# Attention's first two pairs in the written order: 12 fillers, late factors, order kept on four engines

## The chip, the cores and the metric

One NeuronCore of a Trainium2 chip runs the whole program. Its five engines each work through their own instructions in order: PE (TensorE, matrix products and transposes), DVE (VectorE), ACT (ScalarE, here exponentials, copies and casts), POOL (GpSimd) and SP (SyncE, which issues transfers). They wait for each other by semaphores. The metric is the device time of one execution, in microseconds, median of several runs; lower is better.

## The reference

Three layers follow each other, all in float32:

```
scores = (q @ k.T) / sqrt(64), causal         # 4 x 8 heads, 576 tokens of 64
local  = softmax(scores) @ v
phi    = elu(q) + 1
mem    = (phi @ M_prev) / (phi @ z_prev + 1e-6)
g      = sigmoid(beta)                        # one number a head
x      = g * mem + (1 - g) * local            # 2304 tokens x 512
x      = (silu(x @ w_gate) * (x @ w_val)) @ w_out
P      = sinkhorn(x @ moe2_w_gate), 8 rounds  # 8 experts
out    = sum over e of P[:, e] * (relu(x @ w1[e]) @ w2[e])
```

The change touches the attention alone, the first of the three.

## The kernel before

Attention is worked off in pairs of heads, 16 pairs in all. Each float32 operand of a product is split into a high and a low part (QH and QL, KH and KL, and so on), and a product is three products of parts: high with high, high with low, low with high. Keys and queries stand in blocks of 128 columns; because of the causal mask block 4 has scores of 576 columns, block 3 of 448, block 2 of 320 (with block 0, of 64, beside it) and block 1 of 192.

For one pair the work goes through these steps, each a generator that is advanced a piece at a time:

- L, `load`: the transfers of q and k (tile qk), of v and the memory (vm) and of z and q (zq). Then ACT makes QH and KH, POOL the low part KL; then DVE makes QL; then POOL splits the memory (vmr).
- Q, `prepare`: ACT makes the parts of phi (tile ph) in two activations; DVE adds them, multiplies with z (pz), sums (nb) and takes the reciprocal; POOL scales phi by it.
- S, `scores`: PE makes the scores of a block into a tile ps of PSUM, DVE takes the negated maximum (nm), ACT the exponential (tiles P, and E for block 0) with the row sums (sums). Two tiles ps exist, so the scores of a block wait for the exponentials of the block before the last.
- N, `normalize`: DVE makes factors from the sums, POOL scales the exponentials by them.
- V, `transposed`: PE transposes the scaled exponentials and phi into tiles pt of PSUM, of which three exist; ACT or DVE copies them out (T, F, Z).
- W, `values`: PE multiplies with v and the memory into po; ACT copies the result into xacc.

DVE's factors use beta: `gates` loads beta and moe2's gate weights (at the list's place 1) and, in its second half, makes eb, g and the table gs with one exponential on ACT, four operations of 8 columns, ten small copies on DVE, and the split of the gate weights (wgs).

Which piece comes when is a written list. BEGIN stands for the first two pairs and the loads of the third ("S0" is the next piece of scores of pair 0; "X33" is 33 filler products of a mask tile with itself into the unused bank po, which nothing reads). ORDER is one round of the loop, run for pairs 2 to 15, in which pieces of a pair and of its two neighbours are interleaved. END closes. `schedule` joins them.

The list is the order in which the program is written down; a scheduler then orders each engine's instructions itself, unless an instruction is recorded with `keep_in_program_order`. The wrapper class `Ordered` does that for every call on the four engines PE, ACT, DVE and POOL while `self.steady` is true. In the kernel before this is so from the first piece behind BEGIN and one whole ORDER, so from the second round of the loop on; before that the scheduler decides. The early conversions of the next layer's weights (step C) run in attention too.

Behind attention the gated layer begins, with the conversion of its weights on DVE (`load_units`, tied behind attention's last move on DVE), and then the experts' layer, which takes most of the time. Most lines of attention are recorded under line 93, the wrapper's call.

Of the kernel before, what the change touches and what calls it, by code (L numbers as in the profile page):

```python
# [42 lines left out]
ORDER = """  # L43
# [4 lines left out]


BEGIN = """  # L50
    L0 L0 Q0 X33 L1 L0 L0 S0 L2 X5 Q0 S0 S0 X5 S0 X7 X9 Q0 Q0 L1 Q1 L1 K0 X7 L1 S0 X5 Q1 N0 Q0 X7 X7 Q1
    V0 S0 S1 Q1 S1 S1 N0 V0 V0 V0 V0 V0 S1 S1 L2 Q1 L2 V0 W0 N0 W0 V0 V0 V0 S1 L2 V0 N1 N1 N1 W0
"""
END = """
# [1 line left out]
    U-1 U-1 U-1 U-1 U-1 U-1 U-1  # L56
"""

FIRST = 6

COPIES = "AAAAVVAVAVA"

# [1 line left out]
def schedule(n):  # L64

    steps = lambda text, base: [(s[0], base + int(s[1:])) for s in text.split()]
    middle = [(s, i + LAG[s]) for i in range(2, n) for s in ORDER.split() if i + LAG[s] < n]
    return steps(BEGIN, 0) + middle + steps(END, n)


def joined(steps, *counts):

    for n in counts:
        for _ in range(n):
            next(steps)
        yield
# [86 lines left out]
class Kernel:  # L163
# [34 lines left out]
    def attention(self, after=None):  # L198
        tc = self.tc
        nc = self.nc = Ordered(tc.nc, tc, lambda: self.steady)  # L200
        with ExitStack() as st, ExitStack() as first:
            pool = lambda n, b, to=st, **k: to.enter_context(tc.tile_pool(name=n, bufs=b, reuse_waits="tile", **k))

            self.s1, self.s2 = (pool(f"s{n}", n, first, side="right") for n in (1, 2))
            self.a1, self.a2, self.a3, self.a4 = (pool(f"a{n}", n) for n in (1, 2, 3, 4))
            self.pss = pool("pss", 2, space=PSUM)
            self.pst = pool("pst", 3, space=PSUM)
            self.pso = pool("pso", 1, space=PSUM)
            a1 = self.a1
            self.identb = self.s1.tile([P, P], BF16, name="identb")  # L210
            nc.vector.tensor_copy(self.identb, self.ident)

            self.mask = self.s1.tile([P, P], BF16, name="mask")
            nc.gpsimd.memset(self.mask, 0.0)
            nc.gpsimd.affine_select(
                out=self.mask, in_=self.mask, compare_op=ALU.is_ge, fill=MASKED,
                base=0, pattern=[[1, P]], channel_multiplier=-1,
            )
            self.mask0 = self.s1.tile([P, 2, 64], BF16, name="mask0")
            nc.gpsimd.memset(self.mask0, 0.0)  # L220
            for j in range(2):
                self.masked = nc.vector.tensor_copy(self.mask0[0:64, j], self.mask[0:64, 0:64])
            busy = self.pso.tile([P, 512], F32, name="po")

            self.P0 = []
            for n in range(2):
                t = a1.tile([P, 2, D], F32, name=f"P0{n}")
                nc.vector.memset(t, 0.0)
                self.P0.append(t)

            pairs = [(b, hp) for b in range(B) for hp in range(NP)][:self.n_pairs]
            n = len(pairs)
            live = [dict(b=b, hp=hp, P0=self.P0[hp % 2]) for b, hp in pairs]
            early = self.early()
            for p in live:
                p["steps"] = {
                    "L": self.load(p), "Q": self.prepare(p), "S": self.scores(p), "N": self.normalize(p),
                    "V": self.transposed(p), "W": self.values(p),
                }
                if p in live[:2]:  # L240
                    p["steps"]["S"] = joined(p["steps"]["S"], 2, 1, 2, 2, 2)
                if p is live[0]:
                    p["steps"]["V"] = joined(p["steps"]["V"], *10 * [1], 2)
                p["steps"].update({k: p["steps"][v] for k, v in SAME.items()})
                p["steps"]["C"] = early
            done = object()
            steps = schedule(n)
            for nth, (step, at) in enumerate(steps):
                self.steady = len(BEGIN.split()) + len(ORDER.split()) <= nth
                if nth == len(steps) - len(END.split()) and after:  # L250
                    self.ahead = self.load_units()
                    next(self.ahead)
                if nth == 1:
                    gates = self.gates()
                    next(gates)
                if nth == FIRST:
                    with tc.issue_after(self.low_q.ins):
                        next(gates, None)
                if step == "X":
                    for _ in range(at):  # L260
                        nc.tensor.matmul(busy[:, 0:P], self.mask, self.mask, start=True, stop=True)
                else:
                    next(live[at]["steps"][step], done)
            self.nc, self.steady = tc.nc, False
            first.close()
            if after:
                self.open_early(after)

                with tc.issue_after(self.last_exp.ins):
                    for _ in range(2):  # L270
                        next(self.ahead)
                    self.xs = self.split_x(*CHUNKS1[0])
# [1364 lines left out]
```

## Time and profile before

| what | value |
|---|---|
| median of 3 runs | 2102.82 us (2101.58 to 2103.69) |
| profiled execution, own time | 2105.53 us |
| its span, first to last instruction | 2103.7 us |
| PE busy, share of the span | 2067.0 us, 98% |
| DVE busy | 1716.7 us, 82% |
| ACT busy | 974.1 us, 46% |
| POOL busy | 521.4 us, 25% |
| mean granted clock of PE | 0.997 |

Shares of busy time are means over very different stages. The start of the program, the first 50 us of 2100, has to be read from the timelines. PE's clock has two levels here, 2.4 GHz (granted 1.00) and 1.2 GHz (0.50); a stretch between the two held both.

### The profile page before, as it was taken

The page shows a single profiled execution, that of the slowest core. Times are in us where ns is not written, and L with a number is a line of the kernel's source. Part 1 is how long each engine was busy: PE and PEld are TensorE (multiplying, and loading weights), DVE is VectorE, ACT ScalarE, POOL GpSimd, SP SyncE. Part 2 cuts the span into 40 slices and gives each one's busy share as a digit, 9 for nine tenths or more (in the row PEclk, how much of TensorE's full clock was granted, in tenths as well). Part 3 has the DMA queues.
Part 4 walks back from the last instruction along what each step waited for, and adds up shares of the span by engine and source line. Part 5 has one row for each costly group of instructions (what it writes and reads, how often), then busy time and mean ns, then how long its engine had stood idle before and what let it go on. Part 6 is the DMA issues. An engine that isn't in the chain of part 4 may idle for free.

```text
span 2103.7 us, 40585 instructions
## 1 busy us (share of the span) xinstructions
PE 2067.0 (98%) x15848; PEld 1907.4 (91%) x15848; DVE 1716.7 (82%) x3193; ACT 974.1 (46%) x1912; POOL 521.4 (25%) x458
## 2 busy tenths in 40 slices
PE   7999999999999999999999999999999999999999
PEld 5666787877889889999999999999999999999998
DVE  7899899675454668898888888888889888898887
ACT  6999543443333324444434444444444444444432
POOL 6888544000000042122121221212212122121210
PEclk9999999999999999999999999999999999999999
DMA  5342587476587747656566564665647656575564
GB/s 191 111 142 85 186 288 260 142 251 209 170 285 275 271 130 250 209 172 241 167 236 212 169 234 166 232 201 191 230 163 241 204 186 231 167 240 203 183 212 159
DMA packets 123359, 425.77 MB, mean 202 GB/s; under 512 B 13600, under 2 KB 13600, under 8 KB 120096
## 3 DMA queue, kind: packets, MB, share of 16 engines
q1 hardware_dynamic: 121728, 417.93, 59.3%
q10 hardware_dynamic: 1440, 5.24, 0.6%
q8 instruction: 126, 2.06, 0.4%
q14 instruction: 65, 0.53, 0.1%
HBM read 374.36 MB, written 48.76 MB: 201 GB/s over the span
## 4 chain that ended last, share of the span: by engine, by line
PE 71%; DVE 8%; DMA 4%; issue 1%; ACT 1%; SPq 0%; DVEq 0%; ACTq 0%
PE pu L1447 16%; PE pc L1284 15%; PE pq L1447 11%; PE pt L1284 10%; PE po L559 5%; PE pt L1370 4%; PE p L559 3%; PE pc L559 3%; PE pq L559 2%; DMA xr<-xp 2%; PE pt L559 2%; DMA xp<-xl 2%; DVE m L1300 2%; DVE xacc L1453 2%; DVE h L1269 1%; DVE h L1266 1%
## 5 line engine op out<-in xcount | busy, mean ns | idle before, releaser
L1447 PE MATMUL pu<-xl,h 128*128 128x256 f32 x3240 | 424.7, 278 | 2.6 <-DVE xacc L1453 2.1
L1447 PEld LDWEIGHTS pu<-xl,h 128*128 128x128 f32 x3240 | 393.0, 188 | 6.9 <-DVE xacc L1453 3.8
L1284 PE MATMUL pc<-xr,w 128*128 128x256 f32 x3048 | 390.5, 277 | 3.9 <-DMA xr<-xp 3.8
L1284 PEld LDWEIGHTS pc<-xr,w 128*128 128x128 f32 x3048 | 367.3, 188 | 7.2 <-issue 4.4
L1447 PE MATMUL pq<-xl,h 128*128 128x256 f32 x2430 | 317.1, 277 | 0.0
L1447 PEld LDWEIGHTS pq<-xl,h 128*128 128x128 f32 x2430 | 294.1, 188 | 0.4
L1284 PE MATMUL pt<-xr,w 128*128 128x256 f32 x2280 | 291.0, 277 | 0.0
L1268 ACT CAST h<-m 128x512 fp32r<-128x512 f32 (+1 forms) x345 | 190.4, 556 | 200.8 <-DVE m L1300 193.1
L1284 PEld LDWEIGHTS pt<-xr,w 128*128 128x128 f32 x2280 | 274.2, 188 | 0.7
L1453 DVE SCALAR_TENSOR_TENSOR xacc<-pu,Pw,xacc 128x256 f32<-128x256 f32 x540 | 237.1, 475 | 39.3 <-PE pu L1447 39.1
L1291 ACT COPY m<-pc 128x512 f32<-128x512 f32 x192 | 111.9, 583 | 249.6 <-PE pc L1284 245.7
L1453 DVE SCALAR_TENSOR_TENSOR xacc<-pq,Pw,xacc 128x256 f32<-128x256 f32 x405 | 177.5, 474 | 47.0 <-PE pq L1447 47.0
L1269 DVE TENSOR_TENSOR h<-m,h 128x512 fp32r<-128x512 f32 (+1 forms) x345 | 207.4, 625 | 1.5
L1189 POOL TENSOR_TENSOR ws<-raw 128x512 f32<-128x512 f32 x60 | 80.8, 1356 | 507.8 <-DMA raw<-w 165.6
L1265 ACT ACTIVATE h<-m 128x512 fp32r<-128x512 f32 x192 | 121.4, 633 | 172.3 <-DVE m L1296 164.9
L1300 DVE SCALAR_TENSOR_TENSOR m<-m 128x512 f32<-128x512 f32 x240 | 185.5, 773 | 14.2 <-ACT m L1327 10.6
L1296 DVE TENSOR_TENSOR m<-pt,m 128x512 f32<-128x512 f32 x192 | 131.3, 684 | 53.0 <-ACT m L1291 52.2
L559 PE MATMUL p<-xs,gw 128*128 128x512 f32 (+1 forms) x864 | 171.1, 355 | 3.4 <-ACT hf L796 1.3
L559 PEld LDWEIGHTS p<-xs,gw 128*128 128x128 f32 x864 | 142.3, 188 | 30.7 <-DVE hf L797 2.8
L1266 DVE SCALAR_TENSOR_TENSOR h<-m,h 128x512 fp32r<-128x512 f32 x192 | 150.3, 783 | 12.1 <-ACT h L1265 11.7
L1176 POOL TENSOR_TENSOR w<-raw,w 128x512 fp32r<-128x512 f32 x15 | 38.8, 2584 | 428.9 <-ACT w L1175 428.9
L559 PE MATMUL po<-h,ws 128*128 128x512 f32 x576 | 144.4, 391 | 0.2 <-DVE h L817 0.2
(232 smaller groups left out, 2956.9 us busy)
## 6 DMA issues: line engine op xcount, KB each, us to landing
xr<-xp SPq DMA_DIRECT2D x476, 512.0 KB, 4.2
raw<-w SPq DMA_DIRECT2D x64, 512.0 KB, 7.4
gw<-kg SPq DMA_DIRECT2D x24, 1024.0 KB, 7.0
graw<-gvo SPq DMA_DIRECT2D x36, 512.0 KB, 4.4
kg<-gw SPq DMA_DIRECT2D x24, 512.0 KB, 4.2
ws<-ko SPq DMA_DIRECT2D x24, 512.0 KB, 3.9
xp<-xl SPq DMA_DIRECT2D x21, 512.0 KB, 5.2
qk<-qkv SPq DMA_DIRECT2D x16, 640.0 KB, 5.2
```

Source lines behind the costliest of these rows:

```text
L559: self.nc.tensor.matmul(out, lhs[a], rhs[b], start=start and n == 0, stop=stop and n == 2, skip_group_check=shared)
L1265: nc.scalar.activation(hi, src, AF.Relu)
L1266: self.later(1, lambda: nc.vector.scalar_tensor_tensor(lo, src, 0.0, f32(hi), op0=ALU.max, op1=ALU.subtract))
L1268: nc.scalar.copy(hi, src)
L1269: self.later(1, lambda: nc.vector.tensor_sub(lo, src, f32(hi)))
L1284: self.marks[3] = nc.tensor.matmul(out[:, j * HT:(j + 1) * HT], w[:, a, j, k], x[:, b, k], start=start and j + k + n == 0, stop=k + n == 3 ...
L1291: self.marks[1] = nc.scalar.copy(t, src)
L1296: nc.vector.tensor_add(t, a, b)
L1300: relu = lambda out, a, b, op: nc.vector.scalar_tensor_tensor(out, a, 0.0, b, op0=ALU.max, op1=op)
L1370: nc.tensor.matmul(ph[:, j * HT:(j + 1) * HT], w[:, b, j, k], x[:, c, k], start=j + a + k + m == 0, stop=a + k + m == 4, skip_group_check= ...
L1447: nc.tensor.matmul(po[:, c], h[a][:, x, j, c * P:(c + 1) * P], w2[b][:, y, j], start=start and c + j + n == 0, stop=j + n == 3, skip_group ...
L1453: self.marks[2] = nc.vector.scalar_tensor_tensor(acc, po[:, c], self.Pw[:, at, e:e + 1], acc, op0=ALU.mult, op1=ALU.add)
```

## The change

Three edits, all in the start of attention. BEGIN has 12 fillers where it had 33. FIRST, the place in the list at which the second half of `gates` is written, is 18 where it was 6. And `self.steady` is true from the first piece, so that the four engines keep the written order in BEGIN and in the first round of the loop too. One line that sets it is added before the loop.

```
 BEGIN = """
-    L0 L0 Q0 X33 L1 L0 L0 S0 L2 X5 Q0 S0 S0 X5 S0 X7 X9 Q0 Q0 L1 Q1 L1 K0 X7 L1 S0 X5 Q1 N0 Q0 X7 X7 Q1
+    L0 L0 Q0 X12 L1 L0 L0 S0 L2 X5 Q0 S0 S0 X5 S0 X7 X9 Q0 Q0 L1 Q1 L1 K0 X7 L1 S0 X5 Q1 N0 Q0 X7 X7 Q1
     V0 S0 S1 Q1 S1 S1 N0 V0 V0 V0 V0 V0 S1 S1 L2 Q1 L2 V0 W0 N0 W0 V0 V0 V0 S1 L2 V0 N1 N1 N1 W0
 """
-FIRST = 6
+FIRST = 18
             steps = schedule(n)
+            self.steady = True
             for nth, (step, at) in enumerate(steps):
-                self.steady = len(BEGIN.split()) + len(ORDER.split()) <= nth
+                self.steady = True
```

What this does to the engines is seen in the order of their instructions, below for three places. Buffer numbers differ between the two programs, so the same tile has another number.

On DVE, from pair 1's QL to pair 0's first maxima, before:

```order
L93 SCALAR_TENSOR_TENSOR QL<-qk,QH 128x640
L93 RECIPROCAL g_218<-g_218 128x8
L93 TENSOR_REDUCE nb<-pz 128x10
L93 COPY gs<-g_218 64x4
L93 COPY gs<-g_218 128x4 x4
L93 COPY gs<-g_218 64x4
L93 COPY gs<-g_218 128x4 x4
L93 TENSOR_REDUCE nm_256<-ps 128x1
L93 TENSOR_REDUCE nm_258<-ps 128x1
```

and with the change, from behind pair 0's QL to the first copy into gs:

```order
L93 TENSOR_REDUCE nm_215<-ps 128x1
L93 TENSOR_REDUCE nm_217<-ps 128x1
L93 SCALAR_TENSOR_TENSOR ph<-zq,ph 128x640
L93 TENSOR_REDUCE nm_242<-ps 128x2
L93 TENSOR_REDUCE nm_266<-ps 128x1
L93 TENSOR_REDUCE nm_261<-ps 128x2
L93 TENSOR_TENSOR pz<-ph,zq 128x640
L93 TENSOR_SCALAR eb<-eb 128x8
L93 RECIPROCAL g_295<-eb 128x8
L93 TENSOR_SCALAR g_295<-g_295 128x8
L93 RECIPROCAL g_295<-g_295 128x8
L93 COPY gs<-g_295 64x4
```

The two maxima nm of pair 0's 576-column block stand directly behind its QL now, and the factors (eb, g, gs) behind all maxima of pair 0 but the last; pair 1's QL, which stood ahead of gs, stands behind all of it.

On POOL, from pair 0's phi on, before (P_239, P_285, P_310 and P_371 are pair 0's blocks from 576 to 192 columns, P_151 the place of its block 0, E_313 that block's exponentials):

```order
L93 TENSOR_TENSOR ph<-ph,nb 128x640
L93 TENSOR_SCALAR P_239<-P_239,sums 128x576 x2
L93 TENSOR_SCALAR P_285<-P_285,sums 128x448 x2
L93 TENSOR_TENSOR ph<-ph,nb 128x640
L93 TENSOR_TENSOR KL<-qk,KH 128x640
L93 TENSOR_SCALAR P_310<-P_310,sums 128x320 x2
L93 TENSOR_SCALAR P_151<-E_313,sums 64x64 x2
L93 TENSOR_SCALAR P_371<-P_371,sums 128x192 x2
```

and with the change (the same blocks are P_198, P_244, P_269 and P_350, and E_272):

```order
L93 TENSOR_TENSOR KL<-qk,KH 128x640
L93 TENSOR_SCALAR P_198<-P_198,sums 128x576 x2
L93 TENSOR_SCALAR vmr<-vm 128x256
L93 TENSOR_TENSOR vmr<-vm,vmr 128x256
L93 TENSOR_SCALAR P_244<-P_244,sums 128x448 x2
L93 TENSOR_TENSOR ph<-ph,nb 128x640
L93 TENSOR_SCALAR P_269<-P_269,sums 128x320 x2
L93 TENSOR_TENSOR KL<-qk,KH 128x640
L93 TENSOR_TENSOR ph<-ph,nb 128x640
L93 TENSOR_SCALAR P_151<-E_272,sums 64x64 x2
L93 TENSOR_SCALAR P_350<-P_350,sums 128x192 x2
```

The first KL of the lower rows is pair 1's, the second pair 2's. In both orders pair 2's KL and pair 1's phi stand ahead of the scaling of pair 0's E and 192-column block; KL stands behind the 320-column block now, where it stood ahead of it.

On ACT, from the end of pair 0's exponentials on, before (P_413 is pair 1's first block; QH and KH here are pair 2's):

```order
L93 ACTIVATE P_310,sums<-ps,nm_302 128x320 x2
L93 ACTIVATE E_313,sums<-ps,nm_307 128x64
L93 ACTIVATE QH<-qk 128x640
L93 CAST KH<-qk 128x640
L93 ACTIVATE P_371,sums<-ps,nm_369 128x192 x2
L93 COPY T<-pt 128x4x128 x2
L93 ACTIVATE P_413,sums<-ps,nm_430 128x576
```

and with the change, from pair 1's last exponentials (E_482, P_495) to pair 2's first (P_578):

```order
L93 ACTIVATE E_482,sums<-ps,nm_476 128x64
L93 ACTIVATE P_495,sums<-ps,nm_493 128x192 x2
L93 ACTIVATE QH<-qk 128x640
L93 CAST KH<-qk 128x640
L93 COPY T<-pt 128x128
L93 COPY Z_529<-pt 64x64 x2
L93 COPY F_380<-pt 128x64
L93 CAST Z<-pt 128x512
L93 COPY xacc<-po 128x512
L93 ACTIVATE ph<-zq 128x640
L93 ACTIVATE ph<-ph 128x640
L93 ACTIVATE P_578,sums<-ps,nm_595 128x576
```

Pair 2's QH and KH stand behind all of pair 1's exponentials now, before they stood behind pair 0's E. The copy into xacc of pair 0 and both activations of phi stand ahead of pair 2's first exponential.

On SP one load of values (vm) stands earlier and one load of zq later; the transfers are the same.

## Rows read from the trace of the kernel before

**Rows 1.** The page, share of the span by engine: busy us, share, instructions.

```profile
PE 2067.0 (98%) x15848; PEld 1907.4 (91%) x15848; DVE 1716.7 (82%) x3193; ACT 974.1 (46%) x1912; POOL 521.4 (25%) x458
```

**Rows 2.** Busy time by stretch: length, each engine, granted clock, DMA.

```profile
core 0: us, PE busy (x) PEld busy (x) DVE busy (x) ACT busy (x) POOL busy (x), PEclk, DMA share, GB/s
...
18.00:20.00 2.00, 2.00 (x15) 1.18 (x11) 2.00 (x4) 0.23 (x3) 1.02 (x1) 0.53 1.01 410
...
24.00:26.00 2.00, 2.00 (x13) 1.51 (x12) 1.61 (x2) 2.00 (x7) 2.00 (x3) 0.77 0.23 93
...
61.70:74.40 12.70, 12.41 (x100) 8.59 (x102) 10.43 (x22) 12.08 (x35) 11.56 (x16) 1.00 0.40 116
260.00:280.00 20.00, 20.00 (x90) 16.58 (x89) 19.55 (x33) 8.07 (x13) 10.10 (x5) 1.00 0.89 298
```

**Rows 3.** Timeline of PE, start: start us, length us, what, xcount, idle before.

```profile
6.56 0.61 PE L93 MATMUL ps<-KH,QH 64*128 64x288 f32 x2 [6.56 <-ACT KH L93]
7.10 3.70 PE L93 MATMUL po<-mask 128*128 128x128 bf16 x33
10.73 0.61 PE L93 MATMUL ps<-KL,QH 64*128 64x288 f32 x2
11.14 0.37 PE L93 MATMUL ps<-KH,QL 64*128 64x288 f32 x2
...
11.96 2.06 PE L93 MATMUL po<-mask 128*128 128x128 bf16 x34
17.43 0.47 PE L93 MATMUL ps<-KH,QH 64*128 64x448 f32 x2 [3.42 <-ACT P L93]
...
24.71 0.49 PE L93 MATMUL ps<-KH,QH 64*128 64x288 f32 x1
...
25.86 0.61 PE L93 MATMUL pt<-ident,P 128*128 128x128 f32 x4
...
36.32 0.41 PE L93 MATMUL ps<-KH,QH 64*128 64x288 f32 x2
...
48.90 0.40 PE L93 MATMUL ps<-KH,QH 64*128 64x288 f32 x2
```

**Rows 4.** Timeline of DVE, start.

```profile
5.92 0.83 DVE L93 SCALAR_TENSOR_TENSOR QL<-qk,QH 128x640 fp32r<-128x640 f32 x1 [3.85 <-ACT QH L93]
...
13.54 2.32 DVE L93 COPY gs<-g 64x4 f32<-64x4 f32 x10
15.77 1.41 DVE L93 TENSOR_REDUCE nm<-ps 128x1 f32<-128x576 f32 x2
```

**Rows 5.** Timeline of POOL, start.

```profile
6.59 1.56 POOL L93 TENSOR_TENSOR KL<-qk,KH 128x640 fp32r<-128x640 f32 x1 [4.80 <-ACT KH L93]
...
22.25 2.70 POOL L93 TENSOR_SCALAR P<-P,sums 128x576 f32<-128x576 f32 x4 [2.01 <-DVE nb L93]
...
26.69 1.55 POOL L93 TENSOR_TENSOR KL<-qk,KH 128x640 fp32r<-128x640 f32 x1
...
29.60 0.72 POOL L93 TENSOR_SCALAR P<-E,sums 64x64 f32<-64x64 f32 x2
30.41 0.82 POOL L93 TENSOR_SCALAR P<-P,sums 128x192 f32<-128x192 f32 x2
...
43.40 1.26 POOL L93 TENSOR_TENSOR ph<-ph,nb 128x640 f32<-128x640 f32 x1 [0.36 <-DVE nb L93]
```

**Rows 6.** Timeline of ACT, start.

```profile
23.43 0.74 ACT L93 ACTIVATE QH<-qk 128x640 fp32r<-128x640 f32 x1
...
35.93 0.27 ACT L93 COPY T<-pt 128x128 f32<-128x128 f32 x1
...
37.73 0.75 ACT L93 ACTIVATE ph<-ph 128x640 f32<-128x640 f32 x1
39.33 0.74 ACT L93 ACTIVATE P<-ps,nm 128x576 f32<-128x576 f32 x1 [0.84 <-DVE nm L93]
...
40.77 0.58 ACT L93 COPY xacc<-po 128x512 f32<-128x512 f32 x1
```

## The prediction

> **What bounds the kernel now.** I read first the page's share of each engine, then the busy time by stretch, then the timelines of the first 50 us engine by engine. The page has PE busy for 98% of the span [rows 1]. The stretches show where that is true: in a settled round of attention PE works 12.41 of 12.70 us [rows 2], and further on, where the expert weights are converted, DVE is the engine without a gap, 19.55 of 20 us. Both stretches come behind the start, follow it in a fixed order and hold no slack, so a start that ends D us later or earlier moves the end by D. The question is therefore one of place: when do pair 3's first score products, the first that stand in a settled round, begin? Before, at 48.90 us [rows 3].
>
> In the start itself nothing is full. PE runs 33 fillers while KL has long been there (KL ends at 6.59 + 1.56 = 8.15 [rows 5], KL's first product waits until 10.73 [rows 3]), stands still for 3.42 us before 17.43, and then runs at half clock: 0.53 granted of full speed in 18 to 20 us, back at 0.77 in 24 to 26 [rows 2]. The reader is to see in these rows a chain that goes round all four engines: score products (PE), negated maximum (DVE), exponential (ACT), scaling (POOL), transposes (PE). What counts is what stands in front of each link on its engine.
>
> **The change part by part.** Three edits, one effect that matters: in the first two pairs and in the first round of the loop the four engines' instructions now stand as the list BEGIN writes them. I lay the new order on the durations of the rows, link by link.
>
> First maximum. KH is ready as before, at 6.56 PE starts [rows 3]; the fillers are over by then, since they wait for the mask alone: 12 at 3.70/33 = 0.11 each is 1.3 us in time when PE had nothing else, so their removal costs nothing there. KL's products start at 8.15. Five groups of two products follow, four at 11.14 - 10.73 = 0.41 and one at 7.10 - 6.56 = 0.54, plus 0.6 for the last one's own length and 0.1 of masks: the scores stand at about 11.1. DVE has nothing ahead of the maximum any more, where before the ten copies into gs (13.54, 2.32 long) kept it until 15.77 [rows 4]. Gain so far: 4.7 us.
>
> Pair 0's exponentials. From that maximum to the end of the last exponential of this block, behind which QH starts, it took 23.43 - 15.77 = 7.7 us [rows 4, 6]. The order within is nearly the same, so they end at 11.1 + 7.7 = 18.8.
>
> Pair 1's start, where the gain goes. Before, ACT had made pair 1's QH and KH, and DVE the factors, while the first scores were in the making. Now QH and KH stand on ACT behind pair 0's exponential, and on DVE the factors stand between that exponential and pair 1's QL: four small operations (at the 0.23 of a gs copy, 0.9), the ten copies (2.3), wgs (0.2), the sum into nb and QL (0.8 each, as QL's 0.83 [rows 4]). That is 5.0 us, so 23.8 to 24.0; pair 0's sums come next (two small ones, 0.4), then POOL scales the first block (2.70 for four, 0.7 for the first [rows 5]), then PE transposes four blocks (0.61 [rows 3]). Pair 1's first scores: 24.0 + 0.4 + 0.7 + 0.5 = 25.6, against 24.71 before. The 4.7 us are spent, and 0.9 more.
>
> Pair 1 to its last exponential. Before: 35.93 - 24.71 = 11.2 us [rows 3, 6], with pair 3's QH and KH inside (two of 0.74, 1.4 with their overlap), which now come later: 9.8. On the other side PE's scores of 320 and 192 columns now stand behind pair 0's transposes, whose bank of PSUM is given back by ACT only after both 448-column exponentials: four copies and casts of about 0.5 (the 0.58 of a 512-column copy [rows 6]) and eight transposes at 0.15 that were spread over waiting time now stand in line, 3 us. Bounds: 0 (they still hide) and 3; I take 3, since copy, transposes and scores are each behind the other in the new order. End: 25.6 + 9.8 + 3.0 = 38.4.
>
> Pair 2's preparation, now on the path. Before, ACT cast pair 2's QH at 23.43 and POOL made KL at 26.69 [rows 5, 6]; E0's and the 192-column block's scaling followed at 29.60 and 30.41. In the new order QH and KH stand behind pair 1's last exponential, and on POOL, as before, KL and the scaling of phi stand ahead of pair 0's last scalings: what cost nothing while KL was early now holds them. PE has nothing more to do until those are done, as transposes of the 192-column block are next on it. So: QH and KH 1.4, KL 1.55, phi 1.26, E0 twice 0.72, the first 192-column block 0.41 [rows 5]: 38.4 + 5.3 = 43.7. PE has run dry at about 37, a wait of some 6.7 us that the trace of before does not have.
>
> To pair 2's first exponential. Before, from pair 2's scores to the copy of pair 0's output it took 40.77 - 36.32 = 4.45 us [rows 3, 6]; now eight transposes (1.2) and four products of 256 columns (0.6, taken as four transposes) stand ahead of them on PE: 6.2 us, to 49.9. And the exponential, which before stood ahead of that copy (39.33 against 40.77), now stands behind it and behind both activations of phi: 0.58 and two of 0.75, less 0.1 of overlap at neighbours, 1.9 [rows 6]. So 51.8 where it was 39.33: +12.5 us. From here on the order is the settled one, and pair 3 follows at the old distance, 48.90 - 39.33 = 9.6, at 61.4.
>
> The clock. 34 fillers took 2.06 us at full speed, 61 ns each, against 112 ns for the 33 before them [rows 3]: 2.4 and 1.2 GHz. Before, a stretch of 3.42 us without a product was followed by half speed until about 25 us [rows 2, 3]. A wait of 6.7 us will do at least that, so the 6.2 us from 43.7 on run at half clock until it comes back. Bounds: 0 (all of it hidden behind DVE and ACT) and 6.2 (all at half clock and all on the path); at half speed for 6.2 us, about as long as in before, PE does 3.1 us of work and loses 3.1, of which the exponential's wait for the output copy keeps most: I take 2.
>
> The transfers move little: SP issues one load of values earlier and one zq later, and no chain above waits for either.
>
> Sum: -4.7 + 5.6 (pair 1 late by 0.9) + 11.6 (pair 2's exponential late by 12.5) + 2.0 (clock) = +14.5 us. The profiled execution took 2105.5 us round a span of 2103.7, so 2120.0 by its own time; it lay 2.7 above the median of the runs shown, so the median to expect is 2117. Ends of the terms: without the 3.0 and the clock, +9.5; with the whole 6.2 of clock, +18.7.
>
> The Trainium skill (TensorE: Matmul & The Clock Gate, Part 1: The HAM clock gate) has half speed as the state at rest, lifted by the array's own activity. The trace agrees that the first 33 fillers ran at half speed and the next 34 did not. By that rule 21 fewer fillers and longer waits put the lifting off; that is rival A.
>
> **The rivals.** A: PE stays at 1.2 GHz through the whole start and into the first settled rounds. For it: 0.53 granted after a wait of half the length now expected [rows 2]; against it: the settled rounds keep PE at 12.41 of 12.70, and the clock came back by 26 us before. It costs the 6.2 above, 1 to 2 us more in pair 0 and pair 1, and half a round at half speed: +20 to +25, 2123 to 2128.
>
> B, the other side: the wait on POOL never gets to PE, because pair 1's exponentials come early enough. Its place is QH of pair 2 on ACT, its price the 4.7 us kept from the first maximum: 2098. It decides if that QH starts no later than about 29 us, ten before my 38.4, so that E0's scaling is done when PE wants it. For it: the engines are half idle in the start; against it: pair 1's QL cannot come before the factors, and that link alone eats the 4.7.
>
> C: a late start is swallowed where DVE converts weights. If that stretch waited for its loads and not for DVE, it would end at the same time, 2103. Against it: 19.55 of 20 us busy [rows 2], and the loads are issued as DVE frees their tiles.
>
> D: the change does not do what it says, the scheduler's order staying. The rows of the order show that it is another on three engines, so I give it nothing of its own.
>
> **How the numbers follow.** Forecast (new wait on POOL, +9.5 to +18.7): 0.80. A: 0.08. B: 0.05. C: 0.05. The rest, 0.02, lies nearer no change. A measurement of this kernel tells about 0.2%, 4.2 us, from no change. Slower by over that: forecast and A, 0.88. Within it: C and one of the rest, 0.06. Faster: B and one of the rest, 0.06. The likeliest case's own range is 2112 to 2121; the ends are let out by 2 and 1 for queueing that no row shows: 2110 to 2122.
>
> **What would show it.** In the new profile: the first maximum on DVE near 11 us and gs near 20 (right: the first two links); pair 1's first scores on PE between 25 and 27; KL of pair 2 on POOL near 40, and a wait of PE of 5 to 8 us that a POOL scaling ends, about 37 to 44; half clock granted in the stretch behind it; pair 2's first exponential at 50 to 55, behind the copy into xacc; pair 3's first scores at 59 to 65 and rounds of 12.7 us as before; the stretch of DVE's conversions as long as before. If PE has no such wait, or pair 3's scores begin before 55 us, the forecast is wrong in its main step; if they do begin late and the end does not move, C holds.

## The result: slower by 0.71%, and the profile after

| | before | after |
|---|---|---|
| median, six runs of each side by side | 2103.26 us | 2120.70 us |
| ratio, with its 95% interval | | 1.0071 [1.0054, 1.0088] |
| profiled execution, own time | 2105.53 us | 2121.88 us |
| its span | 2103.7 us | 2120.1 us |

The ratio is 14.9 us of 2103 [11.4, 18.5]; the two profiled executions lie 16.4 us apart. The page has the same work as before: PE's busy time grew by 6.4 us against [rows 1], all other engines by 4 at most, up or down.

```profile
PE 2073.4 (98%) x15827; PEld 1910.9 (90%) x15827; DVE 1712.8 (81%) x3193; ACT 974.4 (46%) x1912; POOL 523.6 (25%) x458
```

So the time is waiting, and some slow products: no engine got more to do. From the timeline of PE (start us, length us, engine, line, what, count, idle time before it and what ended it), the rows that answer to [rows 3]:

```profile
8.15 0.61 PE L93 MATMUL ps<-KL,QH 64*128 64x288 f32 x2 [1.03 <-POOL KL L93]
...
24.67 1.11 PE L93 MATMUL pt<-ident,P 128*128 128x128 f32 x4 [3.91 <-POOL P L93]
25.71 0.61 PE L93 MATMUL ps<-KH,QH 64*128 64x288 f32 x2
...
45.73 1.09 PE L93 MATMUL pt<-ident,P 128*128 128x128 f32 x3 [5.38 <-POOL P L93]
...
56.54 0.47 PE L93 MATMUL ps<-KH,QH 64*128 64x448 f32 x2 [1.93 <-ACT P L93]
...
64.96 0.40 PE L93 MATMUL ps<-KH,QH 64*128 64x288 f32 x2
77.64 0.40 PE L93 MATMUL ps<-KH,QH 64*128 64x288 f32 x2
```

Pair 3's first scores, the first inside a settled round, come at 64.96 us where they came at 48.90: 16.06 later, which is the difference of the spans (16.4) within 0.4. Pair 4's follow 12.68 us on. The same row of the kernel before, for use below:

```profile
61.58 0.40 PE L93 MATMUL ps<-KH,QH 64*128 64x288 f32 x2
```

Both pairs are late by the same 16.06. PE has a wait of 5.38 us that it did not have, ahead of 45.73, and POOL's timeline shows what it waits for:

```profile
41.69 1.55 POOL L93 TENSOR_TENSOR KL<-qk,KH 128x640 fp32r<-128x640 f32 x1 [7.85 <-ACT KH L93]
43.20 1.25 POOL L93 TENSOR_TENSOR ph<-ph,nb 128x640 f32<-128x640 f32 x1
44.44 0.72 POOL L93 TENSOR_SCALAR P<-E,sums 64x64 f32<-64x64 f32 x2
45.25 0.83 POOL L93 TENSOR_SCALAR P<-P,sums 128x192 f32<-128x192 f32 x2
```

Pair 0's 192-column block, at 45.25, stands behind E0, that behind phi (43.20), that behind pair 2's KL (41.69), and KL waited 7.85 us for KH. ACT says why KH was late, and what stands ahead of pair 2's first exponential:

```profile
32.44 0.63 ACT L93 ACTIVATE P<-ps,nm 128x448 f32<-128x448 f32 x1 [2.31 <-DVE nm L93]
33.06 0.63 ACT L93 ACTIVATE P<-ps,nm 128x448 f32<-128x448 f32 x1
...
38.14 0.53 ACT L93 ACTIVATE P<-ps,nm 128x320 f32<-128x320 f32 x1 [2.64 <-DVE nm L93]
...
39.85 0.43 ACT L93 ACTIVATE P<-ps,nm 128x192 f32<-128x192 f32 x1
...
40.24 0.75 ACT L93 ACTIVATE QH<-qk 128x640 fp32r<-128x640 f32 x1
...
53.78 0.59 ACT L93 COPY xacc<-po 128x512 f32<-128x512 f32 x1 [5.26 <-PE po L93]
...
55.67 0.72 ACT L93 ACTIVATE P<-ps,nm 128x576 f32<-128x576 f32 x1
```

QH and KH follow at once on pair 1's last exponential (39.85), and the exponential at 55.67 follows on the copy into xacc, for which ACT stood still for 5.26 us, and on phi. DVE at the start, answering to [rows 4]:

```profile
9.98 1.42 DVE L93 TENSOR_REDUCE nm<-ps 128x1 f32<-128x576 f32 x2 [3.28 <-PE ps L93]
...
19.63 2.30 DVE L93 COPY gs<-g 64x4 f32<-64x4 f32 x10
```

Last the stretches (length; busy time of PE, PEld, DVE, ACT, POOL; granted clock; DMA), the last two answering to [rows 2]:

```profile
24.00:26.00 2.00, 1.33 (x6) 1.00 (x8) 1.97 (x5) 1.09 (x5) 2.00 (x3) 0.50 1.02 399
46.00:48.00 2.00, 2.00 (x10) 1.53 (x11) 0.29 (x1) 0.96 (x5) 1.19 (x3) 0.50 0.24 97
58.00:60.00 2.00, 2.00 (x13) 1.34 (x11) 1.78 (x5) 2.00 (x5) 1.00 (x1) 0.50 0.65 167
77.64:90.34 12.70, 12.41 (x101) 8.59 (x100) 10.43 (x22) 12.10 (x35) 11.58 (x16) 1.00 0.37 117
260.00:280.00 20.00, 20.00 (x90) 16.55 (x89) 19.56 (x34) 7.95 (x14) 8.82 (x5) 1.00 0.87 278
```

PE runs at 1.2 GHz at 24 to 26, 46 to 48 and 58 to 60; a settled round is 12.41 of 12.70 us as before, and DVE's conversions fill 19.56 of 20 us as before. So the loss lies in the first 65 us: 16.06 of the 16.4 are there when pair 3 begins.

### The profile page after: what moved, and what is told of

It is laid out like the page before. It is cut to its first block, busy times and chain, and to the rows that moved or that the text cites. A ratio compares the mean times of both kernels' runs of the same rounds, so it can differ in the third digit from the quotient of the medians.

```text
span 2120.1 us, 40534 instructions
## 1 busy us (share of the span) xinstructions
PE 2073.4 (98%) x15827; PEld 1910.9 (90%) x15827; DVE 1712.8 (81%) x3193; ACT 974.4 (46%) x1912; POOL 523.6 (25%) x458
## 4 chain that ended last, share of the span: by engine, by line
PE 67%; DVE 11%; DMA 5%; issue 1%; ACT 1%; SPq 0%; ACTq 0%; DVEq 0%
PE pu L1448 15%; PE pc L1285 14%; PE pq L1448 10%; PE pt L1285 10%; PE po L560 4%; PE pt L1371 4%; PE pc L560 3%; PE p L560 3%; DMA xr<-xp 2%; DVE xacc L1454 2%; PE pq L560 2%; DVE m L1301 2%; DMA xp<-xl 2%; PE pt L560 2%; DVE h L1270 1%; DVE h L1267 1%
```

## The experiments

Eleven kernels. The theories: O, the order kept in BEGIN costs the time by the chain just read; R, the order kept in the loop's first round; C and K, the fillers and the clock; F, the late factors; the rival W of two runs is named with them. "Shift" is how much later than 61.58 pair 4's first scores stand, the first round in which every kernel runs at full clock.

| kernel | ratio to before, 95% interval | in us | pair 3's scores | shift |
|---|---|---|---|---|
| the change | 1.0071 [1.0054, 1.0088] | +14.9 | 64.96 | +16.06 |
| before, 12 fillers | 1.0016 [1.0003, 1.0029] | +3.4 | 53.81 | +5.71 |
| before, late factors | 0.9995 [0.9984, 1.0007] | -1.1 | 49.38 | +1.21 |
| change, 33 fillers, early factors | 1.0079 [1.0059, 1.0099] | +16.6 | 65.72 | +16.84 |
| change, order kept behind BEGIN | 1.0020 [1.0008, 1.0031] | +4.2 | 53.34 | +4.44 |
| before, first round kept | 1.0021 [1.0010, 1.0033] | +4.4 | 52.08 | +4.28 |
| change, order kept in BEGIN alone | 1.0073 [1.0056, 1.0090] | +15.3 | 63.20 | +14.30 |
| change, pair 2's QH, KH early | 1.0065 [1.0049, 1.0080] | +13.7 | 61.03 | +12.13 |
| change, scaling ahead of KL | 1.0037 [1.0022, 1.0052] | +7.8 | 59.62 | +10.72 |
| change, waits filled | 1.0062 [1.0047, 1.0077] | +13.0 | 61.73 | +12.83 |
| before, 80 fillers more | 1.0005 [0.9994, 1.0016] | +1.1 | 52.38 | +3.49 |
| change, three causes away | 1.0042 [1.0026, 1.0058] | +8.8 | 57.08 | +8.17 |

Over all twelve the time follows the shift one for one: time less shift lies between -2.9 and +1.6 us, -0.7 in the mean, and eleven of the twelve shifts lie inside the interval of their time (the twelfth is the run with 80 fillers more). What the start loses, the kernel loses. A shift is read from one profiled execution of its kernel. In these PE's first score products stand between 6.00 and 6.56 us, as the first load of q and k landed, so half a us of a shift can be the load and not the edit.

### Which edit: fillers alone

```
-    L0 L0 Q0 X33 L1 ...
+    L0 L0 Q0 X12 L1 ...
```

> The kernel before with one edit alone: 12 fillers in place of 33. Theory O (the written order kept in the first two pairs costs the time, by pair 2's QH and KH behind pair 1's exponentials): pair 3's first scores within 1 us of the 48.90 of before, since the first maximum waits for the factors on DVE until 15.8 anyway; ratio 0.998 to 1.002. Rival C (the missing fillers leave PE at half speed for longer): pair 3's first scores 5 us or more later, ratio 1.003 or more. Rival F (the late factors cost it) says as O here.

Pair 3's scores came at 53.81, the ratio is 1.0016 [1.0003, 1.0029]: theory O missed, and C had the direction, with less than it asked for (4.9 us of 5, 1.0016 of 1.003). Pair 1's first scores still stand at 24.68, but PE stays at half speed there, from 18.1 to 35.2 us:

```profile
24.68 0.61 PE L93 MATMUL ps<-KH,QH 64*128 64x288 f32 x1
...
36.28 0.36 PE L93 MATMUL ps<-KH,QH 64*128 64x192 f32 x2
```

and so its stretches say:

```profile
24.00:26.00 2.00, 2.00 (x9) 1.67 (x8) 0.71 (x2) 1.22 (x5) 2.00 (x3) 0.50 0.29 116
30.00:32.00 2.00, 2.00 (x11) 1.36 (x10) 1.35 (x2) 0.95 (x2) 1.28 (x4) 0.50 0.40 164
```

The same products, from those scores to pair 1's 192-column scores, take 11.6 us (24.68 to 36.28) without a wait; before it was 7.4 (24.71 to 32.14, full speed from 25). That is 4.2 us of the 5.71; the rest comes at 52 to 56, at half speed once more. So with the scheduler's order the 21 fillers are worth some 5 us of start by way of the clock, which I had priced at nothing. The scheduler also moved other instructions when the fillers went, so this run is not fillers alone on every engine.

### Which edit: late factors alone

```
-FIRST = 6
+FIRST = 18
```

> The kernel before with one edit alone: the second half of the gates at place 18 of the list in place of 6. Theory O (the kept order costs it): the order on each engine is still the scheduler's, which may put the factors where it likes; pair 3's first scores within 1.5 us of 48.90, ratio 0.998 to 1.002. Rival F (factors that come later hold pair 1's QL and pair 0's scaling, and so everything behind): pair 1's first scores 2 us or more later than 24.71, pair 3's 5 us or more later, ratio 1.003 or more. Rival C (fillers and clock) says no change here.

49.38 and 0.9995 [0.9984, 1.0007]: as O said. In the scheduler's order late factors alone cost nothing that can be told, and F falls.

### Which edit: the kept order alone

```
-    L0 L0 Q0 X12 L1 ...
+    L0 L0 Q0 X33 L1 ...
-FIRST = 18
+FIRST = 6
```

> The changed kernel with 33 fillers and the factors at place 6 again, so that of the three edits the kept order stands alone. Theory O: the wait of PE that a scaling on POOL ends is still there (5 us or more, between 37 and 47 us), pair 3's first scores at 62 to 66 where the changed kernel has 64.96; ratio to before 1.005 to 1.009. Rivals C and F (fillers, factors): with both edits undone the start is as before, pair 3's first scores below 55, ratio 0.998 to 1.003.

Pair 3's scores came at 65.72, the ratio is 1.0079 [1.0059, 1.0099], the change's own loss. The wait that a scaling on POOL ends is 5.12 us, ahead of 45.67, as O said. The kept order alone does it, and under it the other two edits together make no difference that can be told (+16.84 against +16.06); what each of them does under it was not run apart.

### Which part of the order

The order kept only from the first round on, with the change's other edits, and with none of them; then the order kept in BEGIN alone:

```
+                self.steady = len(BEGIN.split()) <= nth
```

> The changed kernel with the written order kept on the four engines only behind BEGIN, from the first piece of the loop's first round on; BEGIN itself stands in the scheduler's order again, with 12 fillers and the late factors. Theory O puts the loss into BEGIN (pair 2's QH and KH there): pair 2's QH on ACT at 23 to 27 us again, no wait of PE of over 4 us behind 30 us, pair 3's first scores at 47 to 51; ratio to before 0.998 to 1.003. Rival R (the kept order of the loop's first round costs it, by the copy into xacc and both activations of phi ahead of pair 2's first exponential): pair 2's first exponential 5 us or more later than 39.33, pair 3's scores at 55 or later, ratio 1.003 or more.

> The kernel before with one edit alone: the written order kept on the four engines from the loop's first round on; BEGIN in the scheduler's order, 33 fillers, the factors at place 6. Theory R (the first round's kept order, with the copy into xacc and phi ahead of pair 2's first exponential, costs 1 to 2 us, and half speed did the rest in the kernel with 12 fillers): pair 2's first exponential at 40.5 to 41.5 where it was 39.33, pair 3's first scores at 49.5 to 51, ratio 0.999 to 1.002. Rival (the kept round costs the 4.4 us which the kernel with BEGIN in the scheduler's order had lost): pair 3's scores at 52.5 or later, ratio 1.001 to 1.004.

```
+                self.steady = not len(BEGIN.split()) <= nth < len(BEGIN.split()) + len(ORDER.split())
```

> The changed kernel with the loop's first round in the scheduler's order again, the written order kept in BEGIN alone (12 fillers, late factors). Theory O (BEGIN's order costs it): PE's wait that a scaling on POOL ends is still 4 us or more, pair 2's first exponential stands ahead of the copy into xacc again, and pair 3's first scores come at 60 to 64, ratio to before 1.004 to 1.007. Rival R (the first round's kept order is what costs): pair 3's scores below 55, ratio 1.003 or less.

Both kernels with the first round kept missed their forecasts. In the first, pair 3's scores came at 53.34, between O's 51 and R's 55, with a ratio as O had it and pair 2's first exponential at 44.09, 4.8 us late where R asked for 5. In the second, the exponential came at 42.09 and pair 3's scores at 52.08, both later than theory R had them and the scores earlier than its rival's 52.5, with a ratio as the rival had it. So the kept first round by itself costs some 4 us (+4.28), and the rows of that second kernel show two parts. On ACT:

```profile
40.19 0.59 ACT L93 COPY xacc<-po 128x512 f32<-128x512 f32 x1 [4.18 <-PE po L93]
...
42.09 0.72 ACT L93 ACTIVATE P<-ps,nm 128x576 f32<-128x576 f32 x1
```

on PE:

```profile
42.95 0.47 PE L93 MATMUL ps<-KH,QH 64*128 64x448 f32 x2 [1.93 <-ACT P L93]
```

and by stretch:

```profile
42.00:44.00 2.00, 1.04 (x10) 0.73 (x10) 1.66 (x3) 2.00 (x6) 0.00 (x0) 1.00 0.00 2
46.00:48.00 2.00, 2.00 (x12) 1.67 (x11) 1.85 (x5) 2.00 (x7) 2.00 (x2) 0.50 0.24 94
```

ACT waits 4.18 us for the product that the copy into xacc takes, with pair 2's first exponential behind it, which comes at 42.09 in place of 39.33 [rows 6]. And behind a wait of PE of 1.93 us the clock is at half from 44.4 to 54.6 us, while PE is busy throughout. What that adds is seen in the first of the two kernels (change, order kept behind BEGIN). It has the same wait, and from its end to pair 4's first scores the same instructions in the same order on all four engines, but at full speed:

```profile
44.95 0.47 PE L93 MATMUL ps<-KH,QH 64*128 64x448 f32 x2 [1.93 <-ACT P L93]
```

```profile
46.00:48.00 2.00, 2.00 (x21) 1.51 (x19) 1.93 (x4) 2.00 (x5) 0.59 (x1) 1.00 0.48 126
```

From the end of the wait to pair 4's first scores it takes 21.07 us there (44.95 to 66.02) and 22.91 here (42.95 to 65.86): half speed is 1.8 of the 4.28, and the wait alone does not bring it. That the two kernels lose about the same (+4.44 and +4.28) is chance: the first, with 12 fillers, had half speed earlier, from 19.5 to 33.2 us, and its copy into xacc stands at 42.19, 2.0 later than here.

BEGIN's order alone costs +14.30, nearly the whole; pair 2's exponential stood ahead of the copy again (51.49 against 55.21), as O said. The wait that a scaling on POOL ends came out at 2.10 us, ahead of 45.90, where O had 4 or more: pair 2's scores now stand ahead of it on PE, with waits of their own for KH and KL (1.08 and 1.25 us). The parts do not add up: 14.3 and 4.3 are 18.6, and together they cost 16.1. Where they overlap was not tried.

### The links of the chain, one by one

Pair 2's QH, KH and KL moved ahead of pair 1's scores; then instead the scaling of E0 and the 192-column block moved ahead of KL (second line of BEGIN):

```
-    V0 S0 S1 Q1 S1 S1 N0 V0 V0 V0 V0 V0 S1 S1 L2 Q1 L2 V0 W0 ...
+    V0 S0 L2 S1 Q1 S1 S1 N0 V0 V0 V0 V0 V0 S1 S1 Q1 L2 V0 W0 ...
```

> The changed kernel with one piece moved in the list: pair 2's QH, KH and KL stand right behind pair 0's first transposes and last scores, ahead of pair 1's scores, where they stood behind pair 1's last exponentials. Theory O (PE's wait at 40.3 to 45.7 comes from pair 2's KL on POOL, which waits for KH on ACT): KL starts near 25 and no longer ends that wait, the wait shrinks from 5.4 to 2 to 3 us since the scaling of pair 0's E and 192-column block now waits for phi and its own place only; pair 3's first scores at 60 to 62 instead of 64.96, ratio to before 1.004 to 1.006 where the changed kernel had 1.0071. Rival W (the wait is due to the order of the scalings alone, or to pair 1's long exponentials): the wait stays at 5 us or more and the ratio at 1.007.

```
-    ... S1 S1 L2 Q1 L2 V0 W0 N0 W0 ...
+    ... S1 S1 N0 L2 Q1 L2 V0 W0 W0 ...
```

> The changed kernel with one piece moved in the list: the scaling of pair 0's E and 192-column block on POOL stands ahead of pair 2's QH, KH and KL; QH and KH stay behind pair 1's last exponentials. Theory O (the scaling waits for KL, not for its own data): the wait of PE that ended at 45.73 is gone or under 1.5 us, pair 2's scores then wait for KL (ready near 43.2) instead, so pair 3's first scores come at 60 to 62 in place of 64.96, ratio to before 1.004 to 1.006. Rival W (the scaling's own data are late): wait and ratio stay.

In the first, KL starts at 29.58 (25 was expected) and the wait shrinks from 5.38 to 1.65 us, more than expected, while the ratio, 1.0065, lies just above the 1.006 expected; on POOL the scaling now waits for phi, and phi for DVE:

```profile
29.58 1.54 POOL L93 TENSOR_TENSOR KL<-qk,KH 128x640 fp32r<-128x640 f32 x1
...
38.94 1.71 POOL L93 TENSOR_TENSOR ph<-ph,nb 128x640 f32<-128x640 f32 x1 [5.61 <-DVE nb L93]
```

and on PE:

```profile
41.93 1.09 PE L93 MATMUL pt<-ident,P 128*128 128x128 f32 x3 [1.65 <-POOL P L93]
```

In the second the scaling runs straight behind the 320-column block, and no wait of PE over 0.84 us is left there:

```profile
33.40 0.72 POOL L93 TENSOR_SCALAR P<-E,sums 64x64 f32<-64x64 f32 x2
34.22 0.83 POOL L93 TENSOR_SCALAR P<-P,sums 128x192 f32<-128x192 f32 x2
```

Pair 3's scores at 59.62 and the ratio of 1.0037 are better than expected. The two give back 3.9 and 5.3 us of shift, of which 0.5 and 0.4 are the earlier first load (PE's first scores at 6.02 and 6.11, in the change at 6.51). The wait was made by what stood ahead of the scaling on POOL, not by its data.

### The clock in the new waits

```
-    ... X7 X7 Q1
+    ... X7 X57 Q1
-    ... W0 N0 W0 V0 V0 V0 S1 ...
+    ... W0 N0 W0 H45 V0 V0 V0 S1 ...
...
+                elif step == "H":
+                    for _ in range(at):
+                        nc.tensor.matmul(self.po[:, 0:P], zero, self.mask, start=False, stop=False)
...
```

> The changed kernel with fillers in two of PE's waits: 50 more products of the mask ahead of the wait that ended at 24.67, and 45 products with a zero tile, added into pair 0's output where they add nothing, ahead of the wait that ended at 45.73. No other engine's order moves. Theory K (beside the order, half speed behind the new waits costs 3 to 4 us of the +16): granted clock 1.00 in 24 to 33 and in 46 to 50, pair 3's first scores at 61 to 63.5 in place of 64.96, ratio to before 1.005 to 1.0065. Rival (half speed there lies beside DVE's and ACT's work and costs nothing): clock up, pair 3's scores and the ratio as in the changed kernel, within 0.5 us. If the fillers themselves hold PE up, the scores come later than 64.96.

61.73, as K said; the ratio is 1.0062 [1.0047, 1.0077]. The clock was up in 46 to 50 as expected, but in 24 to 33 only until 29.6. By stretch:

```profile
24.00:26.00 2.00, 1.78 (x18) 1.36 (x18) 1.97 (x4) 1.30 (x5) 2.00 (x3) 1.00 1.06 416
30.00:32.00 2.00, 1.58 (x8) 1.18 (x7) 0.23 (x2) 2.00 (x6) 1.04 (x2) 0.50 0.00 0
46.00:48.00 2.00, 2.00 (x22) 1.28 (x20) 1.50 (x6) 0.40 (x1) 0.49 (x1) 1.00 0.00 0
```

PE from pair 1's first scores on:

```profile
24.80 0.40 PE L93 MATMUL ps<-KH,QH 64*128 64x288 f32 x2
...
44.27 0.84 PE L93 MATMUL pt<-ident,P 128*128 128x128 f32 x3 [2.18 <-POOL P L93]
```

ACT, the two parts of pair 1's stage and the copy:

```profile
30.00 0.64 ACT L93 ACTIVATE P<-ps,nm 128x448 f32<-128x448 f32 x1 [1.59 <-DVE nm L93]
30.63 0.63 ACT L93 ACTIVATE P<-ps,nm 128x448 f32<-128x448 f32 x1
...
36.68 0.53 ACT L93 ACTIVATE P<-ps,nm 128x320 f32<-128x320 f32 x1 [3.38 <-DVE nm L93]
...
50.49 0.59 ACT L93 COPY xacc<-po 128x512 f32<-128x512 f32 x1 [4.09 <-PE po L93]
```

From the end of the wait to the copy it took 6.22 us (44.27 to 50.49), in the change 8.05 (45.73 to 53.78): half speed behind the new wait costs 1.8 us. In pair 1, from the first scores to the 448-column exponentials, it took 5.20 (24.80 to 30.00) at full speed, in the change 6.73 (25.71 to 32.44) at half: 1.5 more. Half speed came back from 29.6 to 39.8, and from those exponentials to the 320-column ones it took 5.42 (31.26 to 36.68), where the change, with full speed from 33.2 to 36.6, had 4.45. So most of what the fillers gave in this stage was lost in it again, to half speed at a later place: from pair 1's first scores to pair 2's QH it took 13.98 (24.80 to 38.78), in the change 14.53 (25.71 to 40.24). Of the 3.2 us by which pair 3's scores came earlier, 0.4 are the earlier first load (6.07 against 6.51).

The other way round, fillers into the wait of the kernel before:

```
-    ... S0 L2 X5 Q0 S0 S0 X5 ...
+    ... S0 L2 X85 Q0 S0 S0 X5 ...
```

> The kernel before with 80 more fillers behind pair 0's first scores, where PE stood still for 3.42 us ahead of 17.43. Theory K (half speed behind such a wait costs time in the start): granted clock near 1.00 in 18 to 25 where it was 0.50, pair 3's first scores 1 to 2 us earlier than 48.90, ratio to before 0.998 to 1.000. Rival (the first 25 us wait for DVE and ACT, whatever PE's clock): no change of pair 3's scores within 0.5 us. The scheduler may put the fillers elsewhere; then the clock of 18 to 25 stays and nothing is learned.

The clock is 1.00 at 18 to 20 and 24 to 26, where it was 0.53 and 0.77 [rows 2], and pair 3's scores still come 3.5 us later, which neither theory had; the ratio is 1.0005 [0.9994, 1.0016]. With the fillers the scheduler had set DVE's, ACT's and POOL's instructions in another order; what full speed alone would be worth before stays open.

### Three causes taken away

The early QH, KH and KL, the early scaling and 50 fillers together:

```
+    ... X7 X57 Q1
+    V0 S0 L2 S1 Q1 S1 S1 N0 N0 V0 V0 V0 V0 V0 S1 S1 Q1 L2 V0 W0 W0 ...
```

> The changed kernel with three causes taken away together: pair 2's QH, KH and KL behind pair 0's first transposes and last scores; the scaling of pair 0's E and 192-column block ahead of phi's; 50 fillers ahead of the wait that ended at 24.67. Theory O with K: alone they gave back 3.9, 5.3 and (with the second set of fillers) 3.2 us of pair 3's first scores. They cover one another in part, so 7 to 10 us together: pair 3's scores at 55 to 58, no wait of PE over 2 us behind 25 us, ratio to before 1.002 to 1.0045; what is left is pair 1's late scaling and the copy into xacc and phi ahead of pair 2's first exponential. Rival (each of them takes away the same wait and another stands behind it): 59 or later, ratio 1.0045 or more.

57.08 and 1.0042 [1.0026, 1.0058], as O with K said. Half of the loss is gone, and behind 28.08 us PE's largest wait is the one of 1.93 us that the change has ahead of 56.54:

```profile
48.10 0.47 PE L93 MATMUL ps<-KH,QH 64*128 64x448 f32 x2 [1.93 <-ACT P L93]
```

The third cause went only in part: the wait that the 50 fillers were to fill is still 2.70 us, ahead of 24.13, and PE is at half speed from 25.2 to 32.0 and from 35.4 to 38.8, and once more from 49.1 to 55.9:

```profile
28.00:30.00 2.00, 1.92 (x10) 1.33 (x11) 0.62 (x2) 0.75 (x3) 2.00 (x3) 0.50 0.57 189
50.00:52.00 2.00, 2.00 (x14) 1.67 (x14) 1.93 (x5) 1.90 (x5) 1.27 (x2) 0.50 0.66 197
```

Of the 8.17 us that are left, 7.9 stand ahead of pair 2's first exponential (47.23, before 39.33). The copy into xacc comes 4.6 later than before (45.34, before 40.77), and the exponential, which before stood 1.4 ahead of it, stands 1.9 behind it, after copy and phi: 3.3. Pair 1's first scores are no later than before (24.72, before 24.71), so the 4.6 arise between them and the copy; how much of that is half speed was not tried.

No kernel here beats the one before; the nearest, late factors alone, can't be told from it.

## Why the prediction was right, and where its sizes were off

The forecast was 2117 us, 2110 to 2122; the median was 2120.7. The wait on POOL, its chain and the late exponential behind copy and phi came as written. Several sizes did not, and some of them came out in the sum by luck. Step by step:

- **First maximum on DVE**, forecast 11.1: 9.98. Five groups of two products and the masks took 1.8 us from 8.15, where I had laid 2.9 on them: 0.41 is the distance from the first group to the second alone, and I took it for all; the next ones stand 0.24 apart (8.56, 8.80, 9.04, 9.28).
- **E's exponential and pair 1's first scores**, forecast 18.8 and 25.6: 18.5 and 25.71. That both fit is luck in part: from the first maximum to the end of E's exponential it took 8.5 us, not the 7.7 carried over from before, which made up for most of the 1.1 above. The gain is spent as written, and gs is at 19.63 (forecast near 20).
- **Pair 1's last exponential**, forecast 38.4: the end is at 40.2. This is the term that was mis-sized: from the first scores on I took 9.8 + 3.0 = 12.8, and it is 14.5. The line of copies, transposes and scores between the 448- and the 320-column exponentials is 4.45 us in the ACT rows above (33.69 to 38.14). Before, it was 0.56 (32.01 to 32.57):

```profile
30.75 0.63 ACT L93 ACTIVATE P<-ps,nm 128x448 f32<-128x448 f32 x1
31.38 0.63 ACT L93 ACTIVATE P<-ps,nm 128x448 f32<-128x448 f32 x1
...
32.57 0.53 ACT L93 ACTIVATE P<-ps,nm 128x320 f32<-128x320 f32 x1 [0.48 <-DVE nm L93]
```

So it is 3.9 more, outside my bounds of 0 and 3. The other part lies ahead of it, from the first scores to the 448-column exponentials: 6.73, before 6.04 (24.71 to 30.75), and 5.20 in the run with the waits filled, at full speed. By that run the new order alone would have made this part 0.8 shorter, which nearly covers the 0.9 that the line took over its bound; half speed added 1.5. It runs from 22.9 to 33.2, from within the wait of 3.91 us ahead of 24.67 that the order also makes. I had charged the clock only behind the wait on POOL.

- **Pair 2's preparation**, forecast 5.3 from there: 40.2 to 45.73, 5.5. The chain QH, KH, KL, phi, E0, scaling is in the rows in that order, and the two runs that moved one link each broke it. PE ran dry at 40.35, not at 37, so the wait is 5.38 us and not 6.7.
- **PE to the copy, and to the exponential**, forecast 6.2 and 1.9, with 2.0 for the clock: 8.05 and 1.89. With the wait filled it was 6.22, so the work was right to 0.1 and the clock behind this wait (1.8) to 0.2. Pair 2's first exponential, at 55.67, lies a little behind the 50 to 55 that I had named as a sign.
- **To pair 3**, forecast 9.6: 9.29. Then rounds of 12.68 us.

Together: 61.4 and 2.0 of clock made 63.4, the trace has 64.96. The 1.6 that are missing are, but for small differences of either sign, the 1.7 of pair 1's stage, and about the size of the half speed there. The sum for the span, +14.5, met +16.4.

**The rivals.** A, half speed until after the first settled rounds, did not come: the clock is full from 60.5 us on. Its ground was there all the same: behind the first 10 us the granted clock has four stretches of half speed in the start of the change where before had one, and the run with 12 fillers alone shows some 17 us of it in one piece. I had written that the fillers' removal "costs nothing there", since PE had nothing else to do; that run is where this failed, +5.7 us. In the kept order it does not show: with 33 fillers and early factors together the kernel is no faster. That the waits hide it there is likely and was not shown. The Trainium skill (TensorE: Matmul & The Clock Gate, Part 1: The HAM clock gate) has full speed as what a busy array gets. These traces do not agree as far as the profile's busy time goes: PE counted as busy for 2.00 of 2.00 us at 0.50 in the run with 12 fillers (30 to 32) and with the first round kept (46 to 48). B needed pair 2's QH by 29 us: moved there by hand (25.80), the kernel still lost 13.7 us and PE still waited 1.65 us for the scaling, so its condition is not enough. C, a late start that the conversions swallow, falls with the table: the shift carries through one for one. D falls too: the order is another one, as the rows say. The kept first round by itself was no rival of mine, only the 1.9 us of copy and phi inside the sum; alone it costs 4 us.

## What to carry to other kernels

Where the settled part holds no slack, find the first instruction that belongs to it and ask only when that one starts: here the same row one round on, where all run at full speed, told the time of twelve kernels to within 3 us. When a scheduler's order is exchanged for a written one, follow each queue past the piece that moves, since the wait appears where something ready stands behind something late; moving one piece gave back 3.9 and 5.3 us here, filling the waits 3.2. And price a wait of PE twice, once for its length and once for the speed of what follows it. The second price was between 0 and 1.8 us here for the same wait, so read it from the trace.

## What the runs showed of the hardware that was not expected

- The same wait of 1.93 us, with the same instructions in the same order behind it, was followed by half speed of different length: none with the order kept behind BEGIN, 57.0 to 60.5 us in the change, 49.1 to 55.9 with three causes away, 44.4 to 54.6 in the kernel before with the first round kept. From the end of the wait to pair 4's first scores these four took 21.07, 21.10, 21.65 and 22.91 us. So 3.4 us of half speed cost nothing there, 6.8 us cost 0.6 and 10.2 us cost 1.8. What decides on the length was not tried.
- Half speed can begin over 1 us behind the end of a wait, not in it: in the kernel before with the first round kept the wait ended at 42.95, and 42 to 44 still shows 1.00. At the waits of 3.91 and 5.38 us in the change it began before the wait ended (at 22.9 and 43.4).
- In the first 10 us the granted clock does not tell the speed: it shows 1.00 in 2 to 4 us of the change, where the 12 fillers took 1.46 us, 122 ns each; at full speed a filler took 61 [rows 3].
